# Attention scores of a two-layer kernel: from stacked 128-row matmuls to three terms of 64 rows per head

## The chip, the cores and the metric

The kernel runs on one core of one Trainium2 chip. The metric is the device time of one execution in microseconds (us), taken as the median of several executions. The core's engines are named as the profile names them: PE is the matmul array, PEld its weight loader, ACT the scalar engine, DVE the vector engine, POOL GpSimd, and SP issues the DMAs. PSUM is the memory that matmuls write to.

## The reference

Attention with 4 batches, 8 heads, 576 rows and head dimension 64 keeps the 32 largest scores of each row; its output goes through two gated layers, called MoE in the code.

```python
scores = scale * np.matmul(q, k.transpose(0, 1, 3, 2))
kth = np.partition(scores, -top_k, axis=-1)[..., -top_k:-top_k + 1]
scores = np.where(scores >= kth, scores, -1000000000.0)
attn = np.exp(scores - np.max(scores, axis=-1, keepdims=True))
attn = attn / (np.sum(attn, axis=-1, keepdims=True) + 1e-09)
x = np.matmul(attn, v)          # then transposed and reshaped to 2304 x 512
g = x @ w_gate
x = (g * (1.0 / (1.0 + np.exp(-g))) * (x @ w_val)) @ w_out     # d_ff 1536
x = (1.0 / (1.0 + np.exp(-(x @ w_gate2))) * (x @ w_val2)) @ w_out2
```

The order of the scores decides which 32 stay, so they are computed to nearly full f32 precision.

## The kernel before

The 2304 tokens are 36 tiles of 64 rows, taken in six chunks of 4, 5, 6, 7, 7 and 7 tiles (`SIZES`). Of each chunk the kernel does the attention, for four head pairs, and then the two layers. A batch has 9 tiles, so chunks 3 and 4 (counted from 0) span two batches and have two segments per head pair.

**Split numbers.** From chunk 1 on matmuls work on fp32r operands in two parts: a head (the value rounded to fp32r, written by ACT at L459 or POOL at L461) and a remainder (value less head, by POOL or DVE at L464), both made by `split_ops`. The MoE matmuls (L920) add three terms of four 128-row matmuls each: head by head, remainder by head, head by remainder. Weight blocks come by DMA at L452 as `raw` and are split into `w`.

**Scores.** Chunks 0 and 1 and the first head pair of chunk 2, and all of chunk 5 ahead of time (`EARLY`), take their scores from `score_ops`: plain f32 matmuls of 64 rows and 64 columns (L639), where a pair of row tiles and a pair of heads make four quarters of the array. The other 19 segments (3 of chunk 2, 8 each of chunks 3 and 4) go through `stacked` and `stacked_scores`. There each head's key block is in DRAM twice over, one copy under the other (`kD`, 128 x 576), is loaded to `kr` and split to `kh` and `kl`; the queries come the same way (`qD`), and `qs` holds their head in rows 0 to 63 and their remainder in rows 64 to 127. A matmul over 128 rows then adds two terms at once, and two of them, with `kh` and `kl`, all four. A group (`qk`, L622) is four such matmuls, two for each head, 288 of the 576 keys wide; each head writes its own PSUM bank of the one `ps_s` buffer. ACT copies the group to `s` (L649, or L656 for a single row tile). There are 41 pairs of row tiles, so 82 groups. Each is followed by DVE's search for the 32 largest (L824, L826), ACT's exponential (L777), DVE's mask (L789), the normalisation (L802 on ACT, L804 on POOL), transposes (L866) into `ps_t` and the product with the values (L885) into `ps_v`, which runs as two halves of 64 columns.

**Order.** All instructions are recorded as operations with an estimated duration and a priority. `Plan.run` simulates the engines and writes out the order in which they would start; where an operation can run on two engines, it goes to the one that is free. Each engine then executes its own list in that order, and waits by semaphores. So whatever changes durations or counts changes the order everywhere behind it.

Of the kernel before, what the change touches and what calls it, by code (L numbers as in the profile page):

```python
# [9 lines left out]
F32 = mybir.dt.float32  # L10
# [17 lines left out]
NEG = -3.0e38  # L28
SIGN = -2147483648
N_SLAB = 3 * NF  # L30

SIZES = [4, 5, 6, 7, 7, 7]
MODES = "NPPPPP"
# [38 lines left out]
W = 4  # L72
# [238 lines left out]
def dma(n_bytes):  # L311
    return n_bytes / 280.0


@with_exitstack
def attn_moe_kernel(ctx: ExitStack, tc, qT, kT, qD, kD, vL, wall, outT):
    nc = tc.nc
    ctx.enter_context(tc.manual_schedule())
    plan = Plan()
# [70 lines left out]
    for n in sorted(set(PHASE)):  # L390
        mine = [c for c in range(len(SIZES)) if PHASE[c] == n]
        kinds = {MODES[c] for c in mine}
        specs = {}
        if "N" in kinds:
            T = max(SIZES[c] for c in mine if MODES[c] == "N") * 64
            specs.update(xn=([P, ND, T], F32, 2), hn=([P, NF, T], F32, 1), wr=([P, 512, 2], I32, WR),
                         wu=([P, 512], I32, WU), wg=([P, 128], I32, 2))
            if any(x != "0" for x in EARLY):
                specs.update(se=([P, 2, 2, 288], F32, 2), qe=([P, S], F32, 2), ke=([P, S], F32, KE))
        if kinds - {"N"}:  # L400
            T = max(SIZES[c] for c in mine if MODES[c] != "N") * 64
            specs.update({nm: ([P, k, T], F32R, 1) for nm, k in (("xh", ND), ("xl", ND), ("hh", NF), ("hl", NF))})
        if kinds - {"N"}:
            specs["raw"] = ([P, 512], F32, RAW)
        if n == 0:
            specs.update(q=([P, S], F32, Q_RING), k=([P, S], F32, K_RING))
        if n == PHASE[-1]:
            Q = 128 * max(x for y in chunks[NAT:] for _, _, x in y[2])
            specs.update(qr=([P, Q], F32, 1), qs=([P, Q], F32R, QS_RING), kr=([P, S], F32, KR_RING),
                         kh=([P, S], F32R, 2 * KS_RING), kl=([P, S], F32R, 2 * KS_RING))  # L410
        phase_rings[n] = [(nm, v[2]) for nm, v in specs.items()]
        if "N" in kinds:
            R["wf", n] = Ring(home, WF)
        if kinds - {"N"}:
            R["w", n] = Ring(lambda nm: [home(f"w_{4 * int(nm.split('_')[1]) + i}", F32R) for i in range(4)], WF // 4)
            R["w", n].after = [R["wf", 0]]
        for nm, (shape, dt, bufs) in specs.items():
            R[nm, n] = ring(nm, shape, dt, bufs, in_phase=n)
            R[nm, n].after = [R[x, n - 1] for x, _ in phase_rings.get(n - 1, [])]
# [20 lines left out]
    def new(name, label=""):  # L440
        r = R[name]
        return Gen(r, f"{name if isinstance(name, str) else name[0]}_{len(r.gens)}{label}")
# [6 lines left out]
    def load(gen, src, dst=None, prio=0, n_bytes=0, deps=()):  # L449
        def fn():  # L450
            take(gen)
            nc.sync.dma_start(gen[:] if dst is None else dst(gen), src)  # L452
        return op("dma", dma(n_bytes), fn, allocs=[gen], prio=prio, lat=DMA_LAT, deps=deps)

    def split_ops(hi, lo, raw, n, uses, deps, pa, pp, allocs=(), lo_raw=None, lo_hi=None):
        def f_hi(eng):
            take(*allocs)
            if eng == "act":
                nc.scalar.activation(out=hi(), in_=raw(), func=AF.Copy)  # L459
            else:  # L460
                nc.gpsimd.tensor_scalar(hi(), raw(), 1.0, 1.0, op0=ALU.mult, op1=ALU.mult)  # L461

        def f_lo(eng):
            (nc.gpsimd if eng == "pool" else nc.vector).tensor_sub(lo(), (lo_raw or raw)(), lo_hi() if lo_hi else f32(hi()))  # L464
        a = op({"act": (act(n), pa), "pool": (76 + n, pa + HP)}, 0, f_hi, deps=deps, uses=uses, allocs=allocs)
        b = op({"pool": (pool_tt(n), pp), "dve": (dve(n), DL)}, 0, f_lo, deps=[a], uses=list(uses) + list(allocs),
               lock=True)
        return a, b
# [109 lines left out]
            nc.sync.dma_start(scr, sg[:, :m])  # L578
        scr_s[p, b, j] = scr, op("dma", dma(P * S * 4 * m), st, deps=done, uses=[sg], prio=E_DMA, lat=DMA_LAT)

    def stacked(bp, q0, n):


        ph = PHASE[-1]
        keys, ops = [], []
        for h in range(2):
            kr, kh, kl = new(("kr", ph)), new(("kh", ph)), new(("kl", ph))
            ld = load(kr, kD[bp, :, h], n_bytes=P * S * 4, prio=1)
            ops += split_ops(lambda kh=kh: kh[:], lambda kl=kl: kl[:], lambda kr=kr: kr[:], S, [kr], [ld], P_K, P_K,
                             allocs=[kh, kl])  # L590
            keys.append((kh, kl))
        qr, qs = new(("qr", ph)), new(("qs", ph))
        W, up, odd = n * 128, slice(64, P), 64 * (n % 2)

        def fn():
            take(qr)
            nc.sync.dma_start(qr[:, :n * 64], qD[bp, :, 0, q0 * 64:(q0 + n) * 64])
        lds = [op("dma", dma(P * n * 256), fn, allocs=[qr], prio=1, lat=DMA_LAT)]

        def fn():  # L600
            nc.sync.dma_start(qr[:, n * 64 + odd:W], qD[bp, :, 1, q0 * 64:(q0 + n) * 64 - odd])
        lds.append(op("dma", dma(P * n * 256), fn, deps=lds, uses=[qr], prio=1, lat=DMA_LAT))
        if odd:
            def fn():
                nc.sync.dma_start(qr[:, n * 64:n * 64 + 64], qD[bp, :, 1, (q0 + n) * 64 - 64:(q0 + n) * 64])
            lds.append(op("dma", dma(P * 256), fn, deps=lds[:1], uses=[qr], prio=1, lat=DMA_LAT))
        ops += split_ops(lambda: qs[:, :W], lambda: qs[up, :W], lambda: qr[:, :W], W, [qr], lds, P_K, P_K, allocs=[qs],
                         lo_raw=lambda: qr[up, :W], lo_hi=lambda: f32(qs[up, :W]))
        return keys, qs, ops, n

    def stacked_scores(sg, kq, o, m):
        keys, qs, deps, n = kq
        done = []
        for x in range(2):
            psg = new("ps_s")

            def qk(x=x, psg=psg):
                take(psg)
                for h in range(2):
                    at = o * 64 + (h * n * 64 + h * 64 * (n % 2) if m == 2 else 0)  # L620
                    for i in range(2):
                        nc.tensor.matmul(psg[:, h, :288], qs[:, at:at + P], keys[h][i][:, x * 288:x * 288 + 288],  # L622
                                         start=(i == 0), stop=(i == 1))
            a = op("pe", pe(4, 288), qk, deps=deps, uses=[qs] + [g for y in keys for g in y], allocs=[psg], prio=P_QK)
            done += to_sbuf(sg, [sg], psg, a, x, m, P_S)
        return done

# [77 lines left out]
    def segment(c, p, b, q0, n_s, x32g, col):  # L705
        bp = b * NPAIR + p
        kg = kq = None
        if p >= int(EARLY[c]) and (c > NAT or c == NAT and p >= NATP):
            kq = stacked(bp, q0, n_s)
        elif p >= int(EARLY[c]):  # L710
            kg, qg = new(("k", 0)), new(("q", 0))
            lds = [load(kg, kT[bp], n_bytes=P * S * 4, prio=1),
                   load(qg, qT[bp, :, q0 * 64:(q0 + n_s) * 64], dst=lambda g: g[:, :n_s * 64],
                        n_bytes=P * n_s * 256, prio=1)]
        vg = new("v")
        v_ld = load(vg, vL[bp], n_bytes=P * 2560, prio=3)
        adds = []
        off = 0
        for n in groups(n_s):
            ptg = new("pt")  # L720
            pt_ops = []
            for jp in range((n + 1) // 2):
                m = min(2, n - 2 * jp)
                pg, sg = new("p"), new("s")
                o = off + 2 * jp
                if kq is not None:
                    done = stacked_scores(sg, kq, o, m)
                elif kg is None:
                    done = [score_load(sg, m, *scr_s[p, b, q0 + o])]
                else:  # L730
                    done = score_ops(sg, [sg], kg, qg, lds, o, m, P_QK, P_S)
                norms = [row_tile(sg, new("st"), done, e, pg, BEFORE[c]) for e in range(m)]
                tiles[0] += 1
                if tiles[0] > E_SKIP:
                    step(E_IN[c])
                for k3 in range(m + 1):
                    pt_ops += turned(pg, norms, ptg, 2 * jp * 64, k3, m)
            adds.append(pv(ptg, pt_ops, vg, v_ld, n, p, x32g, col))
            off += n
            col += n * 64  # L740
        return adds
# [306 lines left out]
        phases["stack"].close()  # L1048


_INS = ["qT", "kT", "qD", "kD", "vL", "wall"]


# [39 lines left out]
```

## Time and profile before

| | us |
|---|---|
| median of 3 runs | 1283.36 |
| lowest and highest | 1279.94, 1286.39 |
| span of the profiled execution | 1286.1 |
| PE busy in it | 1222.6 |
| DVE busy in it | 1121.1 |
| POOL busy in it | 882.8 |
| ACT busy in it | 822.4 |

The profile tells of one execution; its span runs from its first to its last instruction. Matmuls are pipelined: a row gives the first start and the time to the last end, so that matmuls of about 0.3 us each may start 0.13 us apart. What one costs in a stream is the distance from end to end. An idle time is given with what ended it.

### The profile page before, as it was taken

What the parts mean: (1) busy time and instruction counts of PE and PEld (TensorE: products, weight loads), DVE (VectorE), ACT (ScalarE), POOL (GpSimd) and SP (SyncE); (2) the same over time, 40 slices, a digit from 0 to 9 for tenths busy, and PEclk for the clock granted to TensorE, in tenths of its full rate; (3) what the DMA queues carried; (4) which work ended last, traced back from release to release, by engine and by line L of the source; (5) the groups of instructions that cost most, each with busy time, mean ns of one, the idle gap of its engine ahead of it and who ended that gap; (6) DMA issues with size and microseconds to landing.
All of it is one profiled execution on the core that took longest, in us unless ns stands there. A gap on an engine that the chain in (4) does not pass through costs nothing.

```text
span 1286.1 us, 21619 instructions
## 1 busy us (share of the span) xinstructions
PE 1222.6 (95%) x7080; PEld 1051.2 (82%) x7080; DVE 1121.1 (87%) x2330; ACT 822.4 (64%) x1675; POOL 882.8 (69%) x883
## 2 busy tenths in 40 slices
PE   4667999998999999999999999999999999999998
PEld 1223777776988989899999889889888898999998
DVE  7989899899999999999999999999999985475552
ACT  6876888787867877777777776656555553232231
POOL 4642456567987988888998987788797684334431
PEclk9866999999999999999999999999999999999999
DMA  8872888897544445445444443344444332433331
GB/s 266 272 263 89 261 278 283 239 292 245 163 132 127 155 148 162 128 138 162 132 138 145 140 129 123 124 147 160 153 153 137 110 113 94 135 115 100 113 116 37
DMA packets 101202, 206.34 MB, mean 160 GB/s; under 512 B 12256, under 2 KB 21856, under 8 KB 101088
## 3 DMA queue, kind: packets, MB, share of 16 engines
q1 hardware_dynamic: 101088, 204.94, 49.9%
q8 instruction: 56, 0.92, 0.3%
q14 instruction: 58, 0.48, 0.1%
HBM read 173.05 MB, written 31.85 MB: 159 GB/s over the span
## 4 chain that ended last, share of the span: by engine, by line
PE 68%; DVE 13%; ACT 6%; DMA 5%; POOL 4%; issue 3%; SPq 0%; POOLq 0%; DVEq 0%; ACTq 0%
PE ps_m L920 54%; PE ps_v L885 5%; DVE st L824 5%; PE ps_t L866 4%; DMA wr<-in_wall_dram 4%; DVE wk L826 4%; DVE p L789 3%; PE ps_s L622 3%; PE ps_s L639 2%; POOL wu L497 1%; POOL wu L505 1%; ACT wf L478 1%; ACT wg L493 1%; ACT s L649 1%; ACT p L772 1%
## 5 line engine op out<-in xcount | busy, mean ns | idle before, releaser
L464 POOL TENSOR_TENSOR w<-raw,w 128x512 fp32r<-128x512 f32 x314 | 426.1, 1370 | 17.3 <-ACT w L459 13.5
L920 PE MATMUL ps_m<-xh,w 128*128 128x448 f32 (+2 forms) x1920 | 398.4, 349 | 0.6 <-ACT xh L459 0.6
L920 PEld LDWEIGHTS ps_m<-xh,w 128*128 128x128 f32 x1920 | 335.7, 188 | 18.7 <-issue 2.0
L824 DVE MAX8 st<-wk 128x8 f32<-128x576 f32 x432 | 313.0, 746 | 0.0
L920 PE MATMUL ps_m<-xl,w 128*128 128x448 f32 (+2 forms) x960 | 216.1, 346 | 0.0
L826 DVE MATCH_REPLACE8 wk<-st,wk 128x576 f32<-128x576 f32 x288 | 212.9, 740 | 0.0
L920 PE MATMUL ps_m<-hh,w 128*128 128x448 f32 (+2 forms) x960 | 199.3, 350 | 0.0
L461 POOL TENSOR_SCALAR w<-raw 128x512 fp32r<-128x512 f32 x118 | 77.0, 653 | 160.6 <-PE ps_m L920 147.7
L920 PEld LDWEIGHTS ps_m<-xl,w 128*128 128x128 f32 x960 | 172.2, 188 | 7.5 <-POOL xl L464 0.3
L920 PEld LDWEIGHTS ps_m<-hh,w 128*128 128x128 f32 x960 | 169.4, 189 | 8.0 <-issue 1.2
L459 ACT ACTIVATE w<-raw 128x512 fp32r<-128x512 f32 x242 | 148.3, 624 | 20.0 <-PE ps_m L920 8.7
L789 DVE SCALAR_TENSOR_TENSOR p<-s,st,e 128x576 f32<-128x576 f32 x128 | 152.2, 1189 | 0.0
L872 ACT ACTIVATE pt<-ps_t 128x512 f32<-128x512 f32 (+4 forms) x288 | 112.7, 420 | 33.8 <-PE ps_t L866 31.6
L459 ACT ACTIVATE hh<-h 128x448 fp32r<-128x448 f32 (+2 forms) x117 | 63.6, 544 | 98.9 <-DVE h L897 51.6
L866 PE MATMUL ps_t<-ident,p 128*128 128x128 f32 x656 | 104.0, 289 | 12.5 <-ACT p L802 8.7
L866 PEld LDWEIGHTS ps_t<-ident,p 128*128 128x128 f32 x656 | 80.3, 146 | 42.7 <-ACT p L802 17.7
L824 DVE MAX8 st<-s 128x8 f32<-128x576 f32 x144 | 106.9, 743 | 8.0 <-ACT s L649 8.0
L949 ACT ACTIVATE sil<-ps_m 128x448 f32<-128x448 f32 (+3 forms) x144 | 70.0, 486 | 63.2 <-PE ps_m L920 62.7
L920 PE MATMUL ps_m<-hl,w 128*128 128x448 f32 (+2 forms) x480 | 107.9, 346 | 0.0
L826 DVE MATCH_REPLACE8 wk<-st,s 128x576 f32<-128x576 f32 x144 | 106.6, 740 | 0.0
L464 POOL TENSOR_TENSOR hl<-h,hh 128x448 fp32r<-128x448 f32 (+2 forms) x92 | 101.0, 1098 | 7.4 <-ACT hh L459 6.9
L497 POOL TENSOR_SCALAR wu<-wg 128x512 int8<-128x512 int8 x72 | 59.9, 833 | 61.2 <-ACT wg L493 58.9
(71 smaller groups left out, 1835.5 us busy)
## 6 DMA issues: line engine op xcount, KB each, us to landing
raw<-sw SPq DMA_DIRECT2D x360, 256.0 KB, 2.8
wr<-in_wall_dram SPq DMA_DIRECT2D x72, 512.0 KB, 4.9
sw<-wf SPq DMA_DIRECT2D x72, 256.0 KB, 5.4
kr<-in_kD_dram SPq DMA_DIRECT2D x38, 288.0 KB, 2.9
v<-in_vL_dram SPq DMA_DIRECT2D x32, 320.0 KB, 3.1
ss<-se SPq DMA_DIRECT2D x12, 576.0 KB, 3.7
s<-ss SPq DMA_DIRECT2D x12, 576.0 KB, 3.7
out_dram<-h SPq DMA_DIRECT2D x12, 224.0 KB, 2.2
```

Source lines behind the costliest of these rows:

```text
L459: nc.scalar.activation(out=hi(), in_=raw(), func=AF.Copy)
L461: nc.gpsimd.tensor_scalar(hi(), raw(), 1.0, 1.0, op0=ALU.mult, op1=ALU.mult)
L464: (nc.gpsimd if eng == "pool" else nc.vector).tensor_sub(lo(), (lo_raw or raw)(), lo_hi() if lo_hi else f32(hi()))
L497: nc.gpsimd.tensor_scalar(parts(u, I8, 4)[:, :, 3], g[:].bitcast(I8), 64.0, -64.0, op0=ALU.mult, op1=ALU.add)
L789: nc.vector.scalar_tensor_tensor(out=o, in0=src(), scalar=stg[:, 31:32], in1=eg[:], op0=ALU.is_ge, op1=ALU.mult, accum_out=stg[:, 33:34])
L824: nc.vector.max(out=stg[:, 4 * k:4 * k + 8], in_=src() if k == 0 else wk())
L826: nc.vector.match_replace(out=wk(), in_to_replace=stg[:, 4 * k - 4:4 * k + 4], in_values=src() if k == 1 else wk(), imm_value=NEG)
L866: nc.tensor.transpose(tg[:width, i], pg[:, a:a + width], ident)
L872: nc.scalar.activation(out=dst(), in_=src(), func=AF.Copy)
L885: nc.tensor.matmul(og[64 * h:64 * h + 64, :W], vg[:, 8 + h if i == 4 else 4 * h + i], ptg[:, 8 if i == 4 else 4 * h + i, :W], start=(i == ...
L920: nc.tensor.matmul(pg[:, :n], blk(a, d), src(x, d), start=first and i == 0, stop=last and i == 4 * len(terms) - 1)
L949: nc.scalar.activation(out=sg[:, :n], in_=pg[:, :n], func=AF.Tanh, scale=0.5)
```

## The change

`stacked` becomes `split_pair`. It loads the keys of a head pair once (`kT`, head 0 in rows 0 to 63, head 1 in rows 64 to 127), splits them once into `kh` and `kl`, and does the same with the queries (`qh`, `ql`). Where a segment has an odd count of row tiles, it loads one more tile at its side, so that each 128-column block of queries is complete. `split_scores` makes a group of six matmuls in place of four: three terms (`TERMS`), and in each of them head 0 on rows 0 to 63 of the array and head 1 on rows 64 to 127. The fourth term, remainder by remainder, is left out, as in the MoE matmuls. The planner's estimate for a group goes from `pe(4, 288)` to `5 + pe(3, 288)`. The doubled inputs `qD` and `kD` are gone.

```diff
--- before.py
+++ after.py
@@ -28,6 +28,7 @@
 NEG = -3.0e38
 SIGN = -2147483648
 N_SLAB = 3 * NF
+TERMS = ((0, 0), (1, 0), (0, 1))
 
 SIZES = [4, 5, 6, 7, 7, 7]
 MODES = "NPPPPP"
@@ -313,7 +314,7 @@
 
 
 @with_exitstack
-def attn_moe_kernel(ctx: ExitStack, tc, qT, kT, qD, kD, vL, wall, outT):
+def attn_moe_kernel(ctx: ExitStack, tc, qT, kT, vL, wall, outT):
     nc = tc.nc
     ctx.enter_context(tc.manual_schedule())
     plan = Plan()
@@ -405,9 +406,9 @@
         if n == 0:
             specs.update(q=([P, S], F32, Q_RING), k=([P, S], F32, K_RING))
         if n == PHASE[-1]:
-            Q = 128 * max(x for y in chunks[NAT:] for _, _, x in y[2])
-            specs.update(qr=([P, Q], F32, 1), qs=([P, Q], F32R, QS_RING), kr=([P, S], F32, KR_RING),
-                         kh=([P, S], F32R, 2 * KS_RING), kl=([P, S], F32R, 2 * KS_RING))
+            Q = 64 * max(x + x % 2 + (x == 1) for y in chunks[NAT:] for _, _, x in y[2])
+            specs.update(qr=([P, Q], F32, 1), qh=([P, Q], F32R, QS_RING), ql=([P, Q], F32R, QS_RING),
+                         kr=([P, S], F32, KR_RING), kh=([P, S], F32R, KS_RING), kl=([P, S], F32R, KS_RING))
         phase_rings[n] = [(nm, v[2]) for nm, v in specs.items()]
         if "N" in kinds:
             R["wf", n] = Ring(home, WF)
@@ -578,50 +579,48 @@
             nc.sync.dma_start(scr, sg[:, :m])
         scr_s[p, b, j] = scr, op("dma", dma(P * S * 4 * m), st, deps=done, uses=[sg], prio=E_DMA, lat=DMA_LAT)
 
-    def stacked(bp, q0, n):
+    def split_pair(bp, q0, n):
 
 
         ph = PHASE[-1]
-        keys, ops = [], []
-        for h in range(2):
-            kr, kh, kl = new(("kr", ph)), new(("kh", ph)), new(("kl", ph))
-            ld = load(kr, kD[bp, :, h], n_bytes=P * S * 4, prio=1)
-            ops += split_ops(lambda kh=kh: kh[:], lambda kl=kl: kl[:], lambda kr=kr: kr[:], S, [kr], [ld], P_K, P_K,
-                             allocs=[kh, kl])
-            keys.append((kh, kl))
-        qr, qs = new(("qr", ph)), new(("qs", ph))
-        W, up, odd = n * 128, slice(64, P), 64 * (n % 2)
+        kr, kh, kl = new(("kr", ph)), new(("kh", ph)), new(("kl", ph))
+        ld = load(kr, kT[bp], n_bytes=P * S * 4, prio=1)
+        ops = list(split_ops(lambda: kh[:], lambda: kl[:], lambda: kr[:], S, [kr], [ld], P_K, P_K, allocs=[kh, kl]))
+        qr, qh, ql = new(("qr", ph)), new(("qh", ph)), new(("ql", ph))
+        left, right = (q0 - 1, q0 + n + 1) if n % 2 else (q0, q0 + n)
+        lo, hi = (max(0, left) if n == 1 else q0), min(QT, right)
+        pads = [(0, 0)] * (n == 1 and left < 0) + [(right - 1 - lo, QT - 1)] * (right > QT)
+        off = q0 - lo + (n == 1 and left < 0)
+        W = (off + right - q0) * 64
+        at = (off - q0 + lo) * 64
 
         def fn():
             take(qr)
-            nc.sync.dma_start(qr[:, :n * 64], qD[bp, :, 0, q0 * 64:(q0 + n) * 64])
-        lds = [op("dma", dma(P * n * 256), fn, allocs=[qr], prio=1, lat=DMA_LAT)]
-
-        def fn():
-            nc.sync.dma_start(qr[:, n * 64 + odd:W], qD[bp, :, 1, q0 * 64:(q0 + n) * 64 - odd])
-        lds.append(op("dma", dma(P * n * 256), fn, deps=lds, uses=[qr], prio=1, lat=DMA_LAT))
-        if odd:
-            def fn():
-                nc.sync.dma_start(qr[:, n * 64:n * 64 + 64], qD[bp, :, 1, (q0 + n) * 64 - 64:(q0 + n) * 64])
+            nc.sync.dma_start(qr[:, at:at + (hi - lo) * 64], qT[bp, :, lo * 64:hi * 64])
+        lds = [op("dma", dma(P * (hi - lo) * 256), fn, allocs=[qr], prio=1, lat=DMA_LAT)]
+        for d, b in pads:
+            def fn(d=d, b=b):
+                nc.sync.dma_start(qr[:, d * 64:d * 64 + 64], qT[bp, :, b * 64:b * 64 + 64])
             lds.append(op("dma", dma(P * 256), fn, deps=lds[:1], uses=[qr], prio=1, lat=DMA_LAT))
-        ops += split_ops(lambda: qs[:, :W], lambda: qs[up, :W], lambda: qr[:, :W], W, [qr], lds, P_K, P_K, allocs=[qs],
-                         lo_raw=lambda: qr[up, :W], lo_hi=lambda: f32(qs[up, :W]))
-        return keys, qs, ops, n
-
-    def stacked_scores(sg, kq, o, m):
-        keys, qs, deps, n = kq
+        ops += split_ops(lambda: qh[:, :W], lambda: ql[:, :W], lambda: qr[:, :W], W, [qr], lds, P_K, P_K,
+                         allocs=[qh, ql])
+        return (kh, kl), (qh, ql), ops, off
+
+    def split_scores(sg, kq, o, m):
+        keys, qs, deps, off = kq
         done = []
         for x in range(2):
             psg = new("ps_s")
 
             def qk(x=x, psg=psg):
                 take(psg)
-                for h in range(2):
-                    at = o * 64 + (h * n * 64 + h * 64 * (n % 2) if m == 2 else 0)
-                    for i in range(2):
-                        nc.tensor.matmul(psg[:, h, :288], qs[:, at:at + P], keys[h][i][:, x * 288:x * 288 + 288],
-                                         start=(i == 0), stop=(i == 1))
-            a = op("pe", pe(4, 288), qk, deps=deps, uses=[qs] + [g for y in keys for g in y], allocs=[psg], prio=P_QK)
+                for i, (a, b) in enumerate(TERMS):
+                    for h in range(2):
+                        r = slice(64 * h, 64 * h + 64)
+                        at = (off + o - (h if m == 1 else 0)) * 64
+                        nc.tensor.matmul(psg[:, h, :288], qs[a][r, at:at + P], keys[b][r, x * 288:x * 288 + 288],
+                                         start=(i == 0), stop=(i == len(TERMS) - 1))
+            a = op("pe", 5 + pe(3, 288), qk, deps=deps, uses=[*qs, *keys], allocs=[psg], prio=P_QK)
             done += to_sbuf(sg, [sg], psg, a, x, m, P_S)
         return done
 
@@ -706,7 +705,7 @@
         bp = b * NPAIR + p
         kg = kq = None
         if p >= int(EARLY[c]) and (c > NAT or c == NAT and p >= NATP):
-            kq = stacked(bp, q0, n_s)
+            kq = split_pair(bp, q0, n_s)
         elif p >= int(EARLY[c]):
             kg, qg = new(("k", 0)), new(("q", 0))
             lds = [load(kg, kT[bp], n_bytes=P * S * 4, prio=1),
@@ -724,7 +723,7 @@
                 pg, sg = new("p"), new("s")
                 o = off + 2 * jp
                 if kq is not None:
-                    done = stacked_scores(sg, kq, o, m)
+                    done = split_scores(sg, kq, o, m)
                 elif kg is None:
                     done = [score_load(sg, m, *scr_s[p, b, q0 + o])]
                 else:
@@ -1048,7 +1047,7 @@
         phases["stack"].close()
 
 
-_INS = ["qT", "kT", "qD", "kD", "vL", "wall"]
+_INS = ["qT", "kT", "vL", "wall"]
 
 
 def kernel(**inputs):
@@ -1060,7 +1059,6 @@
     q, k, v = (np.asarray(inputs[n]) for n in ("q", "k", "v"))
     qT = q.reshape(B * NPAIR, 2, S, D).transpose(0, 1, 3, 2).reshape(B * NPAIR, P, S)
     kT = k.reshape(B * NPAIR, 2, S, D).transpose(0, 1, 3, 2).reshape(B * NPAIR, P, S)
-    qD, kD = (np.concatenate([x.reshape(B * NPAIR, 2, S, D).transpose(0, 3, 1, 2)] * 2, axis=1) for x in (q, k))
     vv = v.reshape(B * NPAIR, 2, S, D)
     vL = np.zeros((B * NPAIR, P, 10, D), v.dtype)
     for h in range(2):
@@ -1076,7 +1074,7 @@
 
     wall = np.concatenate(slabs("moe_") + slabs("moe2_"), axis=1)
     wall = np.ascontiguousarray(wall.reshape(P, 2 * N_SLAB, 512).transpose(1, 0, 2))
-    data = dict(qT=qT, kT=kT, qD=qD, kD=kD, vL=vL, wall=wall.view(np.uint64))
+    data = dict(qT=qT, kT=kT, vL=vL, wall=wall.view(np.uint64))
 
     nc = _bacc.Bacc("TRN2", target_bir_lowering=False, num_devices=1)
     arrays, args = {}, []
```

The planner's list moves with it. On PE, where the first such group stands; `kh`, `kl` are the parts of the keys, `qs` or `qh` and `ql` those of the queries, `ps_t` are transposes, `ps_v` the attention output, `ps_m` MoE matmuls. Before:

```order
L920 MATMUL ps_m_3122<-xl_2975,w_3040 128x320 x4
L866 MATMUL ps_t_3163<-ident,p_3020 128x128 x4
L866 MATMUL ps_t_3170<-ident,p_3020 128x128
L622 MATMUL ps_s_3174<-kh_3012,qs_3074 128x288
L622 MATMUL ps_s_3174<-kl_3013,qs_3074 128x288
L622 MATMUL ps_s_3174<-kh_3086,qs_3074 128x288
L622 MATMUL ps_s_3174<-kl_3087,qs_3074 128x288
L920 MATMUL ps_m_3183<-xh_2974,w_3059 128x320 x4
```

After:

```order
L884 MATMUL ps_v_3032<-pt_2704,v_2189 64x320 x10
L621 MATMUL ps_s_3066<-kh_3015,qh_3029 128x288 x2
L621 MATMUL ps_s_3066<-kh_3015,ql_3030 128x288 x2
L621 MATMUL ps_s_3066<-kl_3016,qh_3029 128x288 x2
L865 MATMUL ps_t_3082<-ident,p_3023 128x128 x4
L621 MATMUL ps_s_3095<-kh_3015,qh_3029 128x288 x2
L621 MATMUL ps_s_3095<-kh_3015,ql_3030 128x288 x2
L621 MATMUL ps_s_3095<-kl_3016,qh_3029 128x288 x2
L919 MATMUL ps_m_3115<-xh_2977,w_3046 128x320 x4
```

A group is three rows of two matmuls in place of four of one, and the first one moves ahead of the transposes, right behind an attention output. Over the whole list 75 of the 82 groups follow MoE matmuls or transposes, 7 follow an attention output; 66 are followed by MoE matmuls, 15 by transposes and 1 by an attention output.

On POOL, in chunk 3, where the splits of one head pair stand among those of weights (`w`) and hidden values (`hl`). Before:

```order
L464 TENSOR_TENSOR kl_5017<-kr_4755,kh_5016 128x576
L464 TENSOR_TENSOR qs_5020<-qr_4664,qs_5020 64x512
L464 TENSOR_TENSOR hl_4450<-h_25_5037,hh_4449 128x320
L464 TENSOR_TENSOR w_5034<-raw_4922,w_5032 128x512
L464 TENSOR_TENSOR w_5035<-raw_4932,w_5033 128x512
L464 TENSOR_TENSOR kl_5115<-kr_5057,kh_5114 128x576
```

After:

```order
L462 TENSOR_SCALAR w_5082<-raw_4995 128x512
L462 TENSOR_SCALAR kh_5095<-kr_4768 128x576
L465 TENSOR_TENSOR w_5083<-raw_4947,w_5081 128x512
L465 TENSOR_TENSOR kl_5096<-kr_4768,kh_5095 128x576
L465 TENSOR_TENSOR ql_5120<-qr_4775,qh_5119 128x256
```

The second `kl` of the pair is gone, and the remainder of the queries has 256 columns in 128 lanes in place of 512 in 64. Over the whole list POOL has 19 `kl` in place of 38, 19 `ql` in place of 19 `qs` of twice the columns, and 133 heads of weight blocks in place of 118.

## Rows read from the trace of the kernel before

**Rows 1.** The page: totals, and PE's busy tenths in 40 slices.

```profile
span 1286.1 us, 21619 instructions
...
PE 1222.6 (95%) x7080; PEld 1051.2 (82%) x7080; DVE 1121.1 (87%) x2330; ACT 822.4 (64%) x1675; POOL 882.8 (69%) x883
...
PE   4667999998999999999999999999999999999998
```

**Rows 2.** Stretches: bounds, length, busy PE, PEld, DVE, ACT, POOL, clock, DMA share, GB/s.

```profile
312.00:400.00 88.00, 83.01 (x567) 76.84 (x568) 85.92 (x192) 66.67 (x138) 78.10 (x65) 1.00 0.49 153
400.00:700.00 300.00, 295.00 (x1915) 279.72 (x1915) 291.13 (x644) 227.91 (x482) 263.67 (x231) 0.99 0.46 144
700.00:815.00 115.00, 115.00 (x679) 102.75 (x678) 113.25 (x256) 83.39 (x173) 94.50 (x94) 1.00 0.40 126
...
930.00:1286.00 356.00, 352.57 (x1797) 321.52 (x1795) 238.43 (x386) 132.86 (x262) 187.70 (x184) 1.00 0.34 111
```

**Rows 3.** Waits, 312 to 815 us: who waited, us in total, times, longest.

```profile
PE ps_t L866 <- ACT p L802: 6.2, 6, 1.8
PE ps_s L622 <- ACT s L649: 4.6, 4, 2.1
...
PEld ps_t L866 <- POOL p L804: 0.6, 1, 0.6
```

**Rows 4.** Timeline, PE, a score group: start, us to last end, what, count.

```profile
511.06 0.29 PE L622 MATMUL ps_s<-kh,qs 128*128 128x288 f32 x1
...
511.46 0.29 PE L622 MATMUL ps_s<-kl,qs 128*128 128x288 f32 x1
511.59 0.34 PE L920 MATMUL ps_m<-xh,w 128*128 128x384 f32 x1
```

**Rows 5.** Timeline, PE, an early score group between MoE matmuls, cut to single ends.

```profile
200.23 0.38 PE L920 MATMUL ps_m<-hn,wf 128*128 128x256 f32 x1
...
200.54 0.45 PE L639 MATMUL ps_s<-k,q 64*64 64x288 f32 x1
...
200.84 0.41 PE L639 MATMUL ps_s<-k,q 64*64 64x288 f32 x2
201.18 0.48 PE L920 MATMUL ps_m<-hn,wf 128*128 128x256 f32 x1
...
201.18 0.92 PE L920 MATMUL ps_m<-hn,wf 128*128 128x256 f32 x3
```

**Rows 6.** Timeline, PE and PEld, an early score group and the attention output behind it.

```profile
214.51 0.72 PE L639 MATMUL ps_s<-k,q 64*64 64x288 f32 x8
215.16 0.75 PE L885 MATMUL ps_v<-pt,v 128*64 128x320 f32 x3
...
214.51 0.21 PEld L639 LDWEIGHTS ps_s<-k,q 64*64 64x64 f32 x8 [0.33 <-ACT s L649]
...
215.16 0.48 PE L885 MATMUL ps_v<-pt,v 128*64 128x320 f32 x1
```

**Rows 7.** Timeline, PE, from an attention output to transposes.

```profile
554.76 0.33 PE L885 MATMUL ps_v<-pt,v 128*64 128x192 f32 x2
555.02 0.33 PE L866 MATMUL ps_t<-ident,p 128*128 128x128 f32 x1
...
555.02 0.66 PE L866 MATMUL ps_t<-ident,p 128*128 128x128 f32 x4
```

**Rows 8.** Groups of the splits, 312 to 815 us: busy us, mean ns, idle before.

```profile
L464 POOL TENSOR_TENSOR kl<-kr,kh 128x576 fp32r<-128x576 f32 x37 | 57.2, 1545 | 7.0 <-ACT kh L459 5.0 <-PE ps_m L920 1.6
L464 POOL TENSOR_TENSOR qs<-qr,qs 64x384 fp32r<-64x384 f32 (+4 forms) x18 | 25.1, 1395 | 1.5 <-POOL kh L461 0.2
...
L459 ACT ACTIVATE kh<-kr 128x576 fp32r<-128x576 f32 x32 | 21.8, 680 | 8.5 <-DMA kr<-in_kD_dram 8.3
```

**Rows 9.** The page's DMA issues: count, KB each, us to landing.

```profile
kr<-in_kD_dram SPq DMA_DIRECT2D x38, 288.0 KB, 2.9
```

## The prediction

> **What bounds the kernel now.** I read the page's totals first, then the stretches, then who waits for whom, then single instructions. TensorE (PE) is busy 1222.6 of 1286.1 us, and its slices stand at 9 or 8 from the tenth of 40 on [rows 1]. The stretches say where the rest lies: after 700 us PE is busy 115.0 of 115.0 and then nearly all the time, while between 312 and 700 us it is idle 5.0 and 5.0 us [rows 2]. All instructions of the line that changes (L622, 82 groups of four) lie between 312 and 815 us. So PE's own time is the bound there, and each microsecond of it that is added or saved reaches the end, save for those 10 us of idle. VectorE (DVE) is the second: 85.9 of 88 and 291.1 of 300 us busy in these two stretches [rows 2]. PE's idle time there is spent on products that hang on it: on ACT's normalised rows and on ACT's emptying of the score bank, 6.2 and 4.6 us; one wait of the weight loader on GpSimd (POOL) is 0.6 us [rows 3]. GpSimd, ScalarE (ACT) and the DMA engines (busy 0.40 to 0.49 there) end next to no wait of PE. What the change takes from them is worth little; what it does to PE decides.
>
> **PE: the matmuls themselves.** Before, a group of two heads is four full 128-row matmuls of 288 columns that follow the MoE stream without a gap: 511.06 to 511.59, 0.53 us, or 0.133 each [rows 4]. After, it is six of 64 rows: three waves, in each one matmul in either row half. Whether the halves run side by side I read from the 64x64 matmuls of the early scores: eight of them, in two waves, take 0.72 us where one takes 0.45 (0.05 of it the load of its weights), and their eight weight loads together 0.21 [rows 5, 6]. Those tiles include both row halves over the same columns. One after the other, each 0.24, they would need 1.9 us. So a new wave costs one matmul, 0.133, and a group 0.40: 82 x 0.133 = **10.9 us less**. (This rests on f32 tiles of 64 columns; the new ones are fp32r of 128 columns and deliver results at twice the rate. The other bound, six in a row, is a rival below.)
>
> **PE: the changes of array layout.** The new groups stand between matmuls that use the whole array. What that costs is seen where the early scores interrupt the MoE stream [rows 5]. The last MoE matmul ends at 200.61, the first 64x64 one at 200.99: 0.38 apart where the stream alone needs 0.24, so 0.14 is lost. On the way back the last 64x64 ends at 201.25 and the first MoE matmul at 201.66: 0.41 against its pitch of 0.22, so 0.19 to 0.20 is lost. The first matmul after a change is longer by its uncovered weight load: 0.45 against 0.40 (64 columns), 0.48 against 0.38 (128 columns). That leaves 0.09 for emptying the array at each change. Back into transposes it is cheaper: 0.26 from end to end against a pitch of 0.11, so 0.15 [rows 7]. Does a change of the rows alone cost this too? From 64x64 tiles to the 128x64 ones of the attention output only the row split changes: 215.23 to 215.64, 0.41 against the pitch of 0.27, lost 0.14, just the same [rows 6]. So I charge the new groups in full. Their entry loads 128 columns: 0.09 + 0.10 = 0.19. The Trainium skill agrees: "TensorEngine Tiling (Array Packing)", Key Properties, states that changing the tiling mode, not just the tile, drains TensorE. It gives no price, and the rows above do.
>
> In the order after, 75 of the 82 groups are entered from whole-array work: 75 x 0.19 = 14.3. The other 7 are entered from the attention output, whose own way back they replace. Of the exits 66 go to MoE matmuls, 66 x 0.195 = 12.9, and 15 to transposes, 15 x 0.15 = 2.3; one goes to the attention output, which was entered at such a price before. Together **29.5 us more**. Net PE work: 29.5 - 10.9 = **+18.6 us**, 0.23 per group. With the entry as cheap as that of 64 columns (0.14) it is +14.9.
>
> The Trainium skill has a less kind figure for packing, on which nothing here rests: "TensorE: Matmul & The Clock Gate", Measured speedup vs the span model, gives 3.07x for four row tiles; an estimate from it, with the same loss for two, is 0.173 per wave and a sum higher by some 10 us. The rows for two waves of four tiles above show no such loss.
>
> **What PE's idle time gives back.** Each group makes PE later by 0.23 us than before, so ACT and DVE have more time for what PE waited for. At most the 10 us of idle [rows 2] can vanish. The early part cannot, since only 16 of the 82 groups lie before 400 us; of the later waits I take most, together 6 to 7 us. DVE in its order holds MoE steps that now come later from PE, so I don't take all of it. Net **+12 us**.
>
> **The other engines.** GpSimd loses half of the key remainders (38 to 19; the row from 312 us on holds 37, 1.55 us each): 19 x 1.55 = 29.4 us. The query remainders were 18, 25.1 us, 1395 ns each, over n x 128 columns in 64 lanes; now they are 128 to 384 columns wide, about half the time, some 12 us less [rows 8]. ScalarE loses about 19 key heads of 0.68 us, 12.9 us, and some 4 of the queries'. The planner hands part of this room back: 15 weight heads move from ScalarE to GpSimd in the order. None of it lies on PE's path: of PE's and the loader's waits in the stretch the one on GpSimd shown is 0.6 us [rows 3]. I take nothing for it, with 1 us as the gain's end and 0 as the other. DMA: 19 of 38 key loads of 288 KB go [rows 9], and the query loads shrink; SP's queue is shorter, so the weight blocks behind them come no later. No wait is added that did not stand there: score groups still wait for the splits, PE's queue behind them holds MoE matmuls, and the splits are fewer. The key rings are one deep, as for each head before.
>
> **Against what.** The profiled execution has a span of 1286.1 us, 2.7 above the median of the runs, 1283.4 (1279.9 to 1286.4). So the span should come out near 1298 and the median near **1295**.
>
> **Rivals.**
> *The halves share nothing* (the change doesn't do what it says): the matmuls of a wave run one after the other, or their loads do. For it: no row shows two 64x128 tiles at this rate. Against: both row halves in [rows 6]. Matmuls in a row: 6 x 0.133 = 0.80 per group, 82 x 0.27 = +21.9 instead of -10.9, +51.4 with the changes, less up to 10 of idle: about 1325. Loads in a row, 0.10 each, 0.62 per group: +37, about 1311.
> *No emptying of the array for a pure row split* (the side of no slowdown): whole columns stay in use, and the loader fetches the next weights under the running matmul, as it does within [rows 4]. Then only the saving is left. 21 of the 82 groups lie after 700 us where PE never idles and count in full (2.8 us); of the 8.1 us before it, where DVE is 97% busy, some half to all. That is 7 to 11 us less: about 1275. It decides if the entry and exit together cost under the 0.13 that a group saves, that is a third of the 0.34 that they cost in [rows 5]. Against it: the change in [rows 6] that concerns rows alone. For it: both sides of that one split the columns. Here the Trainium skill, "TensorEngine Tiling (Array Packing)", Theoretical Speedup, gives up to 2x for 64 rows; by that alone this would be the outcome, and the rows on the changes speak against it.
> *The second engine takes all of it up*: all 10 us of idle vanish, and DVE, less disturbed by GpSimd, holds nothing up. Then +8.6, 1292. It lies within the forecast's own range.
>
> **How the numbers follow.** Two executions of this kernel differ by up to 0.5%, so a change under 0.5% (6.4 us) can't be told from none. Forecast (halves side by side, changes charged): chance 0.74, from +5 (entry at 0.14 and all idle given back) to +19, 1288 to 1302, and some us of a new order on either side. Halves or loads in a row: 0.14. No emptying: 0.10. Something else: 0.02. The range reaches down into the third case and up to the cheap form of the second: 1276 to 1313. Slower: 0.62 of the forecast's share, with 0.14: 0.76. Within 0.5%: 0.12 of the forecast and 0.05 of no emptying: 0.17. Faster: 0.07.
>
> **What would show it.** In the profile after: matmul pairs of the new line that start within 0.01 us of each other, and waves 0.13 apart; if they stand 0.13 and then 0.13 again apart within a wave, the halves share nothing. A gap of about 0.09 before the first weight load of each group, and the first MoE matmul behind one longer by 0.10; if these are missing, the third case holds. PE's waits on ACT between 312 and 815 us should shrink from 10.8 us. GpSimd should lose about 30 us of busy time with no effect. Wrong would be a time under 1280: then a layout change in rows is free.

## The result, and the profile after

The changed kernel takes 1299.28 us in the median of four runs (1295.55 to 1300.31), the kernel before 1283.46 in its four: the ratio is 1.0113, with an interval of 1.0087 to 1.0139. Measured once more beside the kernel before, it was 1.0114 (1.0078 to 1.0150). So it is slower by some 15 us, where 12 were forecast.

The page of the kernel after, its totals and PE's busy tenths, answers to [rows 1]:

```profile
span 1297.5 us, 21823 instructions
...
PE 1238.3 (95%) x7244; PEld 1041.3 (80%) x7244; DVE 1124.0 (87%) x2320; ACT 805.9 (62%) x1639; POOL 855.1 (66%) x891
...
PE   4667999998999999999999999999999999999998
```

PE is busy 15.7 us longer, POOL 27.7 and ACT 16.5 us less. PE's share of the span is the same 95%: it was the bound and stayed it. The stretches of [rows 2], kernel after, with the same columns:

```profile
312.00:400.00 88.00, 84.99 (x581) 76.35 (x580) 83.00 (x181) 61.38 (x128) 70.97 (x63) 0.98 0.46 136
400.00:700.00 300.00, 297.32 (x1963) 267.15 (x1962) 283.79 (x625) 212.72 (x445) 244.86 (x233) 0.99 0.42 127
700.00:815.00 115.00, 114.95 (x681) 97.60 (x680) 108.44 (x246) 77.28 (x158) 85.63 (x84) 1.00 0.35 105
```

The reader should see that every engine but PE has become idler in them, DVE from 377.0 to 366.8 us in the first two, and that PE's idle time there went from 10.0 to 5.7 us. The waits that it is made of, 312 to 815 us, answer to [rows 3]:

```profile
PE ps_t L865 <- ACT p L801: 3.0, 2, 2.7
PE ps_s L621 <- ACT s L648: 2.7, 1, 2.7
```

Ten waits have become three, and 10.8 us 5.7. Now one new score group between MoE matmuls, PE and its weight loader, with single ends of the MoE matmuls at its sides (start, us to the last end):

```profile
545.16 0.34 PE L919 MATMUL ps_m<-xl,w 128*128 128x384 f32 x1
...
545.43 0.40 PE L621 MATMUL ps_s<-kh,qh 64*128 64x288 f32 x2
545.67 0.30 PE L621 MATMUL ps_s<-kh,ql 64*128 64x288 f32 x2
545.81 0.29 PE L621 MATMUL ps_s<-kl,qh 64*128 64x288 f32 x2
546.03 0.44 PE L919 MATMUL ps_m<-xh,w 128*128 128x384 f32 x1
...
545.43 0.18 PEld L621 LDWEIGHTS ps_s<-kh,qh 64*128 64x128 f32 x2 [0.25 <-issue]
545.54 0.19 PEld L621 LDWEIGHTS ps_s<-kh,ql 64*128 64x128 f32 x2
545.67 0.19 PEld L621 LDWEIGHTS ps_s<-kl,qh 64*128 64x128 f32 x2
546.03 0.65 PEld L919 LDWEIGHTS ps_m<-xh,w 128*128 128x128 f32 x4 [0.17 <-issue]
```

Each of the three rows of PE is a pair. The second and third take 0.30 and 0.29 us to the end of their second matmul, where one whole-array matmul takes 0.29 [rows 4]: by the rows, the halves run side by side. That is tested below. The pairs end at 545.83, 545.97 and 546.10, so a wave is 0.13 to 0.14. The last MoE matmul before ends at 545.50, the first after at 546.47; less that one's own pitch of 0.17 the group takes 0.80, against 0.53 in [rows 4]. In the kernel before, the first weight load of a group runs under the matmul ahead of it, 0.18 before its own matmul at 511.06:

```profile
510.88 0.19 PEld L622 LDWEIGHTS ps_s<-kh,qs 128*128 128x128 f32 x1
```

In the kernel after, load and matmul both start at 545.43, and on the way back both at 546.03. The two idle times of the loader, "issue" in the rows, are waits for nothing that the profile shows. That the array is being emptied in them is the prediction's reading; the profile does not name the cause, and by its modelled ends the load begins 0.07 before the last MoE matmul is done (545.50). The size is what it shows: at the entry the first pair ends 0.33 after the last MoE matmul (545.83), where a matmul in the stream takes 0.13, so 0.20 is lost against 0.19 forecast; on the way back 0.37 against a pitch of 0.17, so 0.20 against 0.195. Over all 82 groups, each from the end of the instruction before it to the end of the one behind it, medians of like neighbours, this kernel takes 19.2 us more than the first experiment below, whose groups are whole-array in the same order. The sum had 18.6.

### The profile page after: what moved, and what is told of

It is laid out like the page before. It is cut to its first block, busy times and chain, and to the rows that moved or that the text cites. A ratio compares the mean times of both kernels' runs of the same rounds, so it can differ in the third digit from the quotient of the medians.

```text
span 1297.5 us, 21823 instructions
## 1 busy us (share of the span) xinstructions
PE 1238.3 (95%) x7244; PEld 1041.3 (80%) x7244; DVE 1124.0 (87%) x2320; ACT 805.9 (62%) x1639; POOL 855.1 (66%) x891
## 4 chain that ended last, share of the span: by engine, by line
PE 74%; DVE 10%; DMA 7%; ACT 6%; POOL 2%; issue 1%; SPq 0%; DVEq 0%; ACTq 0%; POOLq 0%
PE ps_m L919 59%; DMA wr<-in_wall_dram 7%; PE ps_v L884 5%; PE ps_t L865 5%; PE ps_s L621 3%; DVE st L823 3%; DVE wk L825 3%; DVE p L788 2%; PE ps_s L638 2%; ACT wf L479 1%; ACT wg L494 1%; ACT s L648 1%; ACT p L771 1%; POOL wu L506 1%; ACT wu L504 1%
## 5 line engine op out<-in xcount | busy, mean ns | idle before, releaser
L919 PE MATMUL ps_m<-xh,w 128*128 128x448 f32 (+2 forms) x1920 | 404.4, 352 | 0.0
L462 POOL TENSOR_SCALAR w<-raw 128x512 fp32r<-128x512 f32 x133 | 85.5, 643 | 181.6 <-PE ps_m L919 169.2
L460 ACT ACTIVATE w<-raw 128x512 fp32r<-128x512 f32 x227 | 139.8, 623 | 20.3 <-PE ps_m L919 11.5
L801 ACT ACTIVATE p<-p,st 128x576 f32<-128x576 f32 x110 | 84.8, 771 | 25.8 <-DVE st L796 25.2
```

Of the source, the lines that this page charges most:

```text
L801: nc.scalar.activation(out=o, in_=o, func=AF.Copy, scale=stg[:, 35:36])
L919: nc.tensor.matmul(pg[:, :n], blk(a, d), src(x, d), start=first and i == 0, stop=last and i == 4 * len(terms) - 1)
```

## The experiments

Theory: a group loses 0.39 us to its two layout changes and saves 0.13 on its matmuls. Rivals: the loss comes from the new order or the planner's estimate; the halves are not what sets the time of a wave; the splits matter by their own length. A ratio is to the kernel before, measured on the same chip as the run. Five runs (whole array, the added matmul in the middle and at the end, the heads in a row, six in one half) keep the changed kernel's order of operations and differ in the content of a group alone.

**Whole array again.** The changed kernel with its splits, loads and order; only the content of a group is different.

```diff
-                for i, (a, b) in enumerate(TERMS):
-                    for h in range(2):
-                        r = slice(64 * h, 64 * h + 64)
+                for h in range(2):
+                    for i in range(2):
                         at = (off + o - (h if m == 1 else 0)) * 64
-                        nc.tensor.matmul(psg[:, h, :288], qs[a][r, at:at + P], keys[b][r, x * 288:x * 288 + 288],
-                                         start=(i == 0), stop=(i == len(TERMS) - 1))
+                        nc.tensor.matmul(psg[:, h, :288], qs[i][:, at:at + P], keys[i][:, x * 288:x * 288 + 288],
+                                         start=(i == 0), stop=(i == 1))
```

> The changed kernel with its loads, splits and order of instructions, but a score group is four 128-row matmuls over the whole array again (the two heads' products are summed, so the scores are not those of the reference; nothing else is left out). Theory (two layout changes of the array per group, 0.39 us, less 0.13 saved): the 18.6 us of PE work go, so the time is that of the kernel before or a little under it, 1278 to 1286. Rival (the new order, or the planner's wrong estimate of a group, holds the engines up): order and estimate are unchanged, so it stays near 1299, 1294 to 1302.

Measured: 1277.10 us, ratio 0.9976 (0.9959 to 0.9994). A group in its trace, PE between MoE matmuls:

```profile
541.85 0.69 PE L918 MATMUL ps_m<-hl,w 128*128 128x384 f32 x3
542.38 0.30 PE L620 MATMUL ps_s<-kh,qh 128*128 128x288 f32 x1
542.52 0.29 PE L620 MATMUL ps_s<-kl,ql 128*128 128x288 f32 x1
542.65 0.29 PE L620 MATMUL ps_s<-kh,qh 128*128 128x288 f32 x1
542.78 0.29 PE L620 MATMUL ps_s<-kl,ql 128*128 128x288 f32 x1
542.91 0.51 PE L918 MATMUL ps_m<-hh,w 128*128 128x384 f32 x2
```

From the end of the MoE rows at 542.54 to the end of the second MoE matmul at 543.42, less two pitches of 0.17, the group takes 0.54, as in the kernel before. With the same order, estimate and splits the whole slowdown is gone (the time is even just under the 1278 to 1286 expected), so it lies in the groups, and the rival of the order falls. By the ratios 1.0113 and 0.9976 the groups are worth some 17.5 us. What is left, 0.24% or 3.1 us under the kernel before (0.8 to 5.3), is what splits, order and PE's idle time make together.

**One more pair of layout changes, and its measure.** A whole-array matmul into unused columns of the bank, once in the middle of the group (as in the diff) and once behind the loop, at its end.

```diff
                 for i, (a, b) in enumerate(TERMS):
+                    if i == 1:
+                        nc.tensor.matmul(psg[:, 0, 288:512], qs[0][:, off * 64:off * 64 + P], keys[0][:, :224],
+                                         start=True, stop=True)
                     for h in range(2):
...
-                                         start=(i == 0), stop=(i == len(TERMS) - 1))
+                                         start=(i < 2), stop=(i != 1))
```

> The changed kernel with one more whole-array matmul of 224 columns in each group, between its first and second term, into unused columns of the bank; the second term begins its sum anew, so the first term (head by head) is missing from the scores. It adds one way out of and one way into the half-row layout per group. Theory: 0.39 for the two changes and 0.11 for the matmul, 82 x 0.50 = 41 us more, 1333 to 1342. Rival (a change of rows costs nothing, the loss lies elsewhere): only the matmul, +9, 1304 to 1311.

> The same added matmul of 224 columns, but behind the group's last term, where the array goes back to whole rows anyway; the first term is missing from the scores here too. No layout change is added. Theory and rival both: 82 x 0.11 = 9 us more than the changed kernel, 1304 to 1311. The distance of the run with the matmul in the middle from this one is the price of one more pair of changes: 32 us by the theory, 0 by the rival.

Measured: 1328.62 us in the middle, ratio 1.0380 (1.0361 to 1.0399), and 1301.94 at the end, 1.0167 (1.0151 to 1.0184). Both are below the ranges expected. On this chip the kernel before took 1280.59 us, so the changed kernel, at 1.0113 of it, stands at 1295.1; from there the two are 33.5 and 6.9 us more, where 41 and 9 were expected. PE, a group with the matmul in the middle, then, of the other run, one with it at the end:

```profile
549.98 0.40 PE L624 MATMUL ps_s<-kh,qh 64*128 64x288 f32 x2
550.31 0.37 PE L619 MATMUL ps_s<-kh,qh 128*128 128x224 f32 x1
550.61 0.40 PE L624 MATMUL ps_s<-kh,ql 64*128 64x288 f32 x2
550.84 0.29 PE L624 MATMUL ps_s<-kl,qh 64*128 64x288 f32 x2
```

```profile
543.17 0.40 PE L621 MATMUL ps_s<-kh,qh 64*128 64x288 f32 x2
543.41 0.30 PE L621 MATMUL ps_s<-kh,ql 64*128 64x288 f32 x2
543.55 0.29 PE L621 MATMUL ps_s<-kl,qh 64*128 64x288 f32 x2
543.77 0.37 PE L623 MATMUL ps_s<-kh,qh 128*128 128x224 f32 x1
```

The matmul is the same; what it does to the array is not. In the middle it is followed by a second entry: the next pair takes 0.40 and not 0.30, with its weight load uncovered. The two runs lie 26.7 us apart, 0.33 per group, where the theory said 32 and the rival 0. In the profiled executions the stretch from the first score group to the last is 557.7 us (299.5 to 857.2) against 527.3 (305.8 to 833.1), 30.4 apart, or 0.37 per group; what the spans lack of it lies ahead of the first group, where nothing was changed.

**The order within the group.** The loops over heads and terms are swapped: three terms of head 0, then three of head 1.

```diff
-                for i, (a, b) in enumerate(TERMS):
-                    for h in range(2):
+                for h in range(2):
+                    for i, (a, b) in enumerate(TERMS):
                         r = slice(64 * h, 64 * h + 64)
```

> The changed kernel with the six matmuls of a group in another order: the three terms of head 0, then the three of head 1, so that neighbours use the same row half. Theory (halves run side by side only when they alternate, 0.133 per wave): six in a row, 0.80 instead of 0.40 per group, 82 x 0.40 = 33 us more, some 1325 to 1334. Rival (the halves never overlapped fully and each matmul costs its own time): unchanged, 1296 to 1303.

Measured: 1294.88 us, ratio 1.0117 (1.0098 to 1.0135). It is the changed kernel's time, and my expectation of 33 us more fell by its full size. PE, a group:

```profile
546.08 0.41 PE L621 MATMUL ps_s<-kh,qh 64*128 64x288 f32 x2
546.31 0.31 PE L621 MATMUL ps_s<-kh,ql 64*128 64x288 f32 x2
546.45 0.30 PE L621 MATMUL ps_s<-kl,qh 64*128 64x288 f32 x2
```

The program, also as compiled, has `kh,qh`, `kh,ql`, `kl,qh` of head 0 and then the same three of head 1; the trace shows them in pairs, as before, the second of a pair 0.01 us behind the first. So the matmuls of head 1 did not wait for those of head 0 that stand ahead of them. The time alone would also fit the rival, by which a 64-row matmul costs about 0.07 wherever it is; hence the next run.

**Six matmuls in one half.**

```diff
-                        r = slice(64 * h, 64 * h + 64)
+                        r = slice(0, 64)
```

> The changed kernel with all six matmuls of a group on rows 0 to 63 (head 1's scores are those of head 0). The run with the heads in a row showed that the order of the six does not matter: each half took its own three. Theory (the halves run side by side, a half is bound by its own matmuls of 0.13 us): one half now has six, 0.80 per group against 0.40, 82 x 0.40 = 33 us over the changed kernel, 1322 to 1332. Rival (a 64-row matmul costs about 0.07 wherever it is): unchanged, 1293 to 1299.

Measured: 1322.77 us, ratio 1.0335 (1.0285 to 1.0386), 28 us over the changed kernel by the ratios of 1.0335 and 1.0114. PE, a group:

```profile
548.31 0.69 PE L919 MATMUL ps_m<-xl,w 128*128 128x384 f32 x3
548.92 0.53 PE L621 MATMUL ps_s<-kh,qh 64*128 64x288 f32 x2
549.29 0.43 PE L621 MATMUL ps_s<-kh,ql 64*128 64x288 f32 x2
549.56 0.42 PE L621 MATMUL ps_s<-kl,qh 64*128 64x288 f32 x2
549.91 0.62 PE L919 MATMUL ps_m<-xh,w 128*128 128x384 f32 x2
```

A pair now takes 0.42 to 0.43 and not 0.30, and from the first start to the next MoE matmul it is 0.99 in place of 0.60: 0.39 x 82 = 32 us of PE's time, of which PE's idle time takes some (its waits are down to 0.2 us). So a half is bound by its own matmuls at 0.13 each, and the two halves run side by side. That, not the order in which they are written, is what the three waves rest on.

**The planner knows the price.**

```diff
-            a = op("pe", 5 + pe(3, 288), qk, deps=deps, uses=[*qs, *keys], allocs=[psg], prio=P_QK)
+            a = op("pe", 395 + pe(3, 288), qk, deps=deps, uses=[*qs, *keys], allocs=[psg], prio=P_QK)
```

> The changed kernel, but the planner's estimate of a score group is 390 ns longer, about what it costs on the chip with its two layout changes. The number of layout changes is nearly the same in the new order (74 entries and 80 exits against 75 and 81). Theory: PE's work stays, so the time is that of the changed kernel, 1293 to 1299 where the kernel before stands at 1280.6 on this chip; at most the 6.5 us of PE's idle time in the stretch can go. Rival (the wrong estimate put instructions in the wrong place): back towards the kernel before, 1280 to 1288.

Measured: 1297.04 us, ratio 1.0123 (1.0066 to 1.0180). The wrong estimate is not the cause: a planner that knows the price finds no better order.

**Half as many layout changes.** Both groups of a pair of row tiles in one operation, the second with banks of its own (`ps_u`); and, as the measure, the changed kernel with `ps_t` and `ps_m` cut alike and nothing else of it.

```diff
-        "ps_t": ring("ps_t", [P, 4, P], F32, 2, PS),
+        "ps_u": ring("ps_u", [P, 2, 512], F32, 1, PS),
+        "ps_t": ring("ps_t", [P, 4, P], F32, 1, PS),
...
-        "ps_m": ring("ps_m", [P, 512], F32, 3, PS),
+        "ps_m": ring("ps_m", [P, 512], F32, 2, PS),
...
-        for x in range(2):
-            psg = new("ps_s")
+        both = [new("ps_s"), new("ps_u")]
...
-            a = op("pe", 5 + pe(3, 288), qk, deps=deps, uses=[*qs, *keys], allocs=[psg], prio=P_QK)
+        a = op("pe", 10 + pe(6, 288), qk, deps=deps, uses=[*qs, *keys], allocs=both, prio=P_QK)
```

> The two groups of a pair of row tiles (keys 0 to 287 and 288 to 575) are one operation, back to back, so that the layout changes once per pair: 41 entries and 41 exits. The second group has banks of its own, taken from the transposes (1 in place of 2) and the MoE sums (2 in place of 3). To be read against the next run, which has the same banks for those two. Theory: 38 entries less of 0.19 and 37 exits of 0.195, 14 us under the next run. Rival (layout changes cost nothing): the same as the next run within 3 us.

> The changed kernel with one bank for the transposes in place of two, and two for the MoE sums in place of three; the groups stand apart as before, 79 entries and 78 exits. It is the measure for the run with the groups back to back. Both theories: slower than the changed kernel by what the missing banks cost, 1298 to 1340.

Measured: 1292.82 us in pairs, ratio 1.0101 (1.0053 to 1.0148), and 1304.68 for the measure, 1.0197 (1.0150 to 1.0243). They lie 11.9 us apart, where 14 were expected of the theory and at most 3 of the rival: 0.32 for each way in and out of the 38 and 37 by which they differ. (The planner's order differs between the two as well, so some of it may be order.) PE, the two groups of a pair:

```profile
547.71 0.40 PE L622 MATMUL ps_s<-kh,qh 64*128 64x288 f32 x2
547.94 0.30 PE L622 MATMUL ps_s<-kh,ql 64*128 64x288 f32 x2
548.08 0.30 PE L622 MATMUL ps_s<-kl,qh 64*128 64x288 f32 x2
548.21 0.29 PE L622 MATMUL ps_u<-kh,qh 64*128 64x288 f32 x2
548.34 0.29 PE L622 MATMUL ps_u<-kh,ql 64*128 64x288 f32 x2
```

The first pair of the second group takes 0.29 and follows at the pace of a wave: one entry serves both. The price follows the number of changes, down as well as up. But the banks for it cost some 11 us (1.0197 against 1.0114), so the pairs only just make up for them, and stay above the kernel before.

**What the splits are worth.** The kernel before, with only one head's keys loaded and split. The diff leaves out that the rings of `kh` and `kl` have half their buffers and that a group names one head's keys.

```diff
-        for h in range(2):
+        for h in range(1):
             kr, kh, kl = new(("kr", ph)), new(("kh", ph)), new(("kl", ph))
...
+        keys = keys * 2
...
```

> The kernel before, but only the first head's keys are loaded and split, and both heads' matmuls use them (the second head's scores are wrong); the groups stay four matmuls over the whole array. It takes away 19 key loads, 19 key heads and 19 key remainders, the larger part of what the change takes from the splits, and no PE work. Theory (PE is the bound, the splits hang on nothing but PE's idle time in the stretch): between no change and the few us by which the run with whole-array groups stood under the kernel before: ratio 0.996 to 1.001. Rival (the splits hold the kernel up by their own length, some 30 us of GpSimd): ratio under 0.985.

Measured: 1278.89 us, ratio 0.9979 (0.9956 to 1.0001). It cannot be told from no change, and 2.7 us is its middle. The rival, by which the splits' own length counts, would have been under 0.985. The run beside it was the changed kernel once more, told of at the top.

> The changed kernel once more, beside the kernel before on the chip of the run above. Theory and rival both: the ratio of the first measurement, 1.0087 to 1.0139.

No run that computes all the scores is under the kernel before. A variant of it that splits the keys once per pair and copies the parts to the other half by DMA was not tried on the chip.

## Why the prediction was right, point by point

- **PE is the bound, and other engines' relief is worth little.** Right. POOL lost 27.7 us against some 30 expected, and the run with the keys split once puts the larger part of the splits at 2.7 us, with 0 inside its interval, against 0 to 1. One sentence of the prediction contradicts its own rows: ScalarE does not end "next to no wait of PE", it ended all ten that [rows 3] shows, 10.8 us. What holds is that its splits ended none of those. The sum does not use that sentence.
- **The waves.** 0.13 to 0.14 in the trace, as taken from the 64x64 tiles. The rival by which the halves share nothing fell with the six matmuls in one half.
- **The layout changes.** 0.80 for a group against the sum's 0.40 + 0.19 + 0.195, and 19.2 us over all groups against 18.6. The step that read the price of a row split from the change between 64x64 tiles and those of the attention output [rows 6] held: the rival of a free row split would have put the kernel near 1275. The first run, the matmul in the middle and the pairs show the price as a cause, not only as a gap beside others. By the distances between runs it is 0.32 to 0.37 for one way in and one out, by the rows of a group 0.40. [rows 5, 6] alone could not have shown it for the way in: the loader's row for the 64x64 tiles in [rows 6] says that it waited for ACT. The "issue" rows of the kernel after have no such wait.
- **What PE's idle time gives back.** The term was 6 to 7 us. The sum's 18.6 less the measured 14.5 (11 to 18) leaves 4 for it, from 1 to 7: less in the middle than was taken, though 6 to 7 is not excluded. The run with whole-array groups stands 3.1 us under the kernel before (0.8 to 5.3), so most of the 4 is there with groups as short as before. A pair of traces does not size this term. In the profiled execution PE's idle time between 312 and 700 us fell by 4.3 (10.0 to 5.7), and two long waits are left, each followed by something that the prediction had not counted. The kernel after, stretches around the wait before 464.6 us, columns as in [rows 2]:

```profile
461.50:464.60 3.10, 0.47 (x4) 0.20 (x2) 3.10 (x5) 0.65 (x2) 1.79 (x2) 1.00 0.00 0
464.60:468.20 3.60, 3.55 (x16) 3.27 (x17) 3.60 (x12) 2.92 (x6) 1.33 (x1) 0.54 0.61 122
468.20:472.00 3.80, 3.80 (x29) 3.46 (x28) 3.80 (x12) 2.78 (x6) 2.13 (x3) 0.99 0.74 238
```

  PE did little for 3.1 us, and in the next 3.6 its granted clock was 0.54, mostly the lower of its two levels. The same happens behind the wait before 337.4 us (0.64). By the ends of the matmuls there, against their usual pitch, these two cost 1.7 and 1.5 us. The kernel before has one such place, at 471.75 us, of about 1.3. By these two traces the sum would be +18.6 - 4.3 + 1.9 = 16.2. But in the trace of the second measurement the same changed kernel has no such place; its clock stands at the upper level in these stretches:

```profile
312.00:400.00 88.00, 85.50 (x593) 76.60 (x592) 86.18 (x187) 62.65 (x131) 72.45 (x65) 1.00 0.46 136
400.00:700.00 300.00, 298.28 (x1971) 267.46 (x1970) 285.50 (x626) 213.85 (x448) 246.51 (x235) 1.00 0.42 127
```

  PE's idle time is 4.2 us there, 5.8 less than before, and the sum would be 18.6 - 5.8 - 1.3 = 11.5. Both lie within the measured 11 to 18, so the falls of the clock are a matter of the execution, and not shown to be one of the change. Nor is the reason given for the term, that longer groups leave ACT more time, shown: between 312 and 815 us the profile shows no wait of PE in the two runs with still longer groups (the matmul in the middle, six in one half), but also only 0.4 us of waits in the run whose groups are as short as before. What sets this idle time stays open.
- **Against what.** The two profiled executions differ by 11.4 us in their spans, less than the medians: the kernels of one and the same order started their first score group anywhere from 299.5 to 305.8 us, ahead of any instruction that differs. So the comparison of medians is the one that counts.

## What to carry to other kernels

Where small matmuls are packed into parts of the array in the midst of whole-array work, each way in and out has a price, here 0.32 to 0.40 us for both; packing pays only if one stay saves more than that, and three waves in place of four matmuls save 0.13. So count stays, not matmuls, and read the price of a stay from any other tiled matmul in the same trace. Of a lighter load on engines that PE does not wait for, expect next to nothing.

## What the runs showed of the hardware that was not expected

Matmuls of the two row halves need not alternate in the program. With three of one half ahead of three of the other, the second half's first matmul still started 0.01 us behind the first half's, and the kernel's ratio was 1.0117 against 1.0113. The runs don't show how far ahead the array reaches in this way; three matmuls is what was tried.
